# Loading q and k as runs of consecutive tokens over all 128 partitions, nine full transposes each

## The chip, the cores and the metric

One core of one Trainium2 chip runs the whole kernel. The metric is device time in microseconds (us). The kernel before takes 833.95 us, the median of 3 runs (833.22 to 834.21).

## What is computed

Attention over q, k and v of shape (batch 4, heads 8, 576 tokens, head size 64), then a mixture of 8 experts that takes one expert for each token, then a two-layer feed-forward block. Half of the heads look back over 32 tokens (local), the other half at every 32nd token (strided):

```python
scores = scale * np.matmul(q, k.transpose(0, 1, 3, 2))
mask_local = (rel >= 0) & (rel < 32)
mask_strided = (rel >= 0) & (pos[None, :] % 32 == pos[:, None] % 32)
masks = np.stack([mask_local if h < H // 2 else mask_strided for h in range(H)])
attn = softmax(np.where(masks, scores, -1e9))
x = (attn @ v) as rows of tokens               # 2304 x 512
x = _moe_ref(x)                                # top expert of 8, 512 -> 1024 -> 512
out = np.maximum(x @ w_in, 0) ** 2 @ w_out     # 512 -> 2048 -> 512
```

All of it is float32. The change touches the attention alone, which fills the first 165 us of the execution.

## The kernel before

The attention goes batch by batch. `load(b)` issues the transfers of a batch from SyncE's queue (SP): `qs` and `ks` (the four strided heads), `ql` and `kl` with their tails `qlt` and `klt` (the four local heads), `vsp` and `vl` (v for the strided and the local heads). The tiles of q and k have one buffer each, so the next batch's can be loaded only once this batch's have been transposed. `load(1)` is issued ahead of the first batch's scores, and `load(b + 2)` after batch b.

`transposes(b, t)` turns q and k so that the head size lies on the partitions, which the scores need. It yields in 13 groups. A group is a few transposes on TensorE (PE) into one PSUM tile of the pool "tp", which has two buffers, and then one or two copies (`evac`) to `qsT`, `ksT`, `qlT` or `klT`, in turn on ScalarE (ACT) and VectorE (DVE). PSUM tiles are named `ts<b>q`, `ts<b>k` for the strided heads and `tp<b>q`, `tp<b>k`, `tpt<b>` for the local ones. The groups of batch b + 1 are drawn one by one between the units of batch b, by the table `TN`; those of batch 0 at the start.

In `qs` each of 72 partitions holds one head and one run of 32 consecutive tokens (8 KB); in `ql` the tokens lie across the partitions, so that a run in memory is one token's 64 numbers (256 bytes). `piece_s` multiplies, for one residue of the 32, an 18 by 18 block of scores for each head; its PSUM tile is `sc<b>s`. The local units write `sc<b>l`. Behind the scores come the softmax on DVE and ACT (`nm`, `pr`, `sm`, `rc`), another transpose (`pt`), the product with v (`o`) and its copy to `xT`, then the gates (`rw`, `xr`), and stores of x to memory (`x_d`).

The program's order on each engine is set by a scheduler when it is built; each engine then works through its own list in order.

Of the kernel before, what the change touches and what calls it, by code (L numbers as in the profile page):

```python
# [7 lines left out]
F32 = mybir.dt.float32  # L8
# [116 lines left out]
def moe_kernel(ctx, tc, q, k, v, wg, wog, w1, w2, w_in64, w_out64, consts, out, dbg=None):  # L125
# [77 lines left out]
    def turned(pool, i):  # L203
        trs[i] = {}
        for nm in "qk":
            trs[i][nm + "sT"] = pool.tile([P, STRIDE // 2, 4 * SM], F32, name=f"{nm}sT{i}")
            trs[i][nm + "lT"] = pool.tile([P, 2, S], F32, name=f"{nm}lT{i}")

    def padded_v(pool, i):
        vsp[i] = pool.tile([P, 4, 8 * HD], F32, name=f"vsp{i}")  # L210
        nc.gpsimd.memset(vsp[i], 0.0)

    R = 4 * SM
    for nm in "qk":
        qks[nm] = fro.tile([R, STRIDE * HD], F32, name=f"{nm}s")
    turned(fro, B % 2)
    padded_v(big, (B - 1) % 3)
    turned(big, (B - 1) % 2)
# [14 lines left out]
    def load(b):  # L233
        t = {}
        go = nc.sync.dma_start
        if b == 0:
            go = lambda o, i: tc.keep_in_program_order(nc.sync.dma_start(o, i))
        for nm, src in (("q", q), ("k", k)):
            go(qks[nm], src[b, 4:8].rearrange("h (m c) d -> (h m) (c d)", c=STRIDE))
        for nm, src in (("q", q), ("k", k)):  # L240
            x = fro.tile([P, NU, 4, HD], F32, name=f"{nm}l{b}", tag=nm + "l", bufs=1)
            for h in range(4):
                go(x[:, :, h, :], src[b, h, : NU * P].rearrange("(u p) d -> p u d", p=P))
            y = fro.tile([QB, 4, HD], F32, name=f"{nm}lt{b}", tag=nm + "lt", bufs=1)
            go(y, src[b, 0:4, NU * P :].rearrange("h p d -> p h d"))
            t[nm + "l"] = (x, y)
        t["vs"] = x = vsp[b % 3]
        rows = v[b, 4:8].rearrange("h (m i a) d -> i m h (a d)", i=NG, a=8)
        for i in range(NG):
            go(x[32 * i : 32 * i + SM], rows[i])  # L250
        vl = io.tile([KW, 4, NQB, HD], F32, name=f"vl{b}", tag="vl")
        nc.gpsimd.memset(vl[:STRIDE, :, 0, :], 0.0)
        go(vl[STRIDE:, :, 0, :], v[b, 0:4, 0:QB, :].rearrange("h p d -> p h d"))
        for h in range(4):
            base = v[b, h, QB - STRIDE : 2 * QB, :]
            src = bass.AP(base.tensor, base.offset, [[HD, KW], [QB * HD, NQB - 1], [1, HD]])
            last_ld[0] = go(vl[:, h, 1:, :], src)
        t["vl"] = vl
        return t
# [13 lines left out]

    def transposes(b, t):
        t.update(trs[b % 2])
        for c4 in range(STRIDE // 8):
            for nm in ("q", "k"):
                yield
                ps = pss.tile([P, 4, P], F32, name=f"ts{b}{nm}{c4}", tag="tp")
                for i in range(4):  # L280
                    c = (4 * c4 + i) * 2 * HD
                    nc.tensor.transpose(ps[:, i, :R], qks[nm][:, c : c + 2 * HD], ident[:R, :R])
                evac(t[nm + "sT"][:, 4 * c4 : 4 * c4 + 4, :], ps[:, :, :R], 0.125 if nm == "q" else None)
        for hp in range(2):
            for nm in ("q", "k"):
                yield
                ps = pss.tile([P, NU, P], F32, name=f"tp{b}{nm}{hp}", tag="tp")
                for u in range(NU):
                    src = t[nm + "l"][0][:, u, 2 * hp : 2 * hp + 2, :]
                    nc.tensor.transpose(ps[:, u, :], src.rearrange("p h d -> p (h d)"), ident)  # L290
                evac(t[nm + "lT"][:, hp, : NU * P], ps.rearrange("d u p -> d (u p)"), 0.125 if nm == "q" else None)
        yield
        ps = pss.tile([P, 2, 2, QB], F32, name=f"tpt{b}", tag="tp")
        for i, nm in enumerate(("q", "k")):
            for hp in range(2):
                src = t[nm + "l"][1][:, 2 * hp : 2 * hp + 2, :].rearrange("p h d -> p (h d)")
                nc.tensor.transpose(ps[:, i, hp, :], src, ident[:QB, :QB])
        evac(t["qlT"][:, :, NU * P :], ps[:, 0], 0.125)
        evac(t["klT"][:, :, NU * P :], ps[:, 1])

    nun = [0]

# [50 lines left out]
    def piece_s(b, t, u, a):  # L353

        nm = f"{b}s{u}"
        nun[0] += 1
        if a == 0:
            scs[b, u] = pss.tile(G, F32, name=f"sc{nm}", tag="sc")
            nc.tensor.matmul(
                flat(scs[b, u]),  # L360
                identb,
                cstb[:, None, C_MS - C_BF : C_MS - C_BF + SM].to_broadcast([P, n_s, SM]),
                start=True,
                stop=False,
            )
        sc = scs[b, u]
        r = slice(u * HD, (u + 1) * HD)
        for i in range(NG):
            for h in range(4):
                ql, kr = (t[x + "sT"][r, 4 * i + a, SM * h : SM * (h + 1)] for x in "qk")  # L370
                ins = nc.tensor.matmul(sc[32 * h : 32 * h + SM, a, i, :], ql, kr, start=False, stop=(a == i == 3))
        if b == u == 0:
            lead["s0"] = ins
# [369 lines left out]
            scq.append((nun[0] + (SDL if t < GROUPS[1][1] else 0) + i * SCN, lambda i=i, t=t: scatter(i, t)))  # L743

    tg = transposes(0, tiles[0])
    for _ in range(2 * 4 + 1):
        next(tg)
    tiles[1] = load(1)
    nc.gpsimd.memset(zero, 0)
# [3 lines left out]
    for b in range(B):  # L753
        t = tiles[b]
        tn = transposes(b + 1, tiles[b + 1]) if b + 1 < B else iter(())
        for n, ku in enumerate(ORDER[b].split()):
            kind, u = ku[0], int(ku[1:])
            if kind == "l":
                for _ in tg:
                    pass  # L760
                q2.append((b, t, kind, u) + unit(b, t, kind, u))
            else:
                if kind == "b":
                    with tc.issue_after(lead["s0"].ins):
                        next(tg, None)
                piece_s(b, t, "ab".index(kind), u)
                if u == 3:
                    q2.append((b, t, "s", "ab".index(kind)) + unit_s(b, t, "ab".index(kind)))
            drain(D2, D3)
            if b == B - 1 and n >= LN and "do" in lead:  # L770
                lead.pop("do")()
                lead["ok"] = 1
            if b == B - 1 and not early and all(a[0] == b for a in q2 + q3):
                front.close()
                early.append(
                    bulk.enter_context(tc.tile_pool(name="early", bufs=1, side="right", reuse_waits="tile"))
                )
            if scq and nun[0] >= scq[0][0] and (b < B - 1 or "ok" in lead):
                with tc.issue_after(last_ev["p"].ins):
                    scq.pop(0)[1]()  # L780
            for _ in range(TN[b][n]):
                next(tn, None)
        for _ in tn:
            pass
        tg = iter(())
        if b + 2 < B:
            tiles[b + 2] = load(b + 2)
# [649 lines left out]
```

## Time and profile before

| | |
|---|---|
| median of 3 runs | 833.95 us |
| the profiled execution's own time | 826.2 us |
| its span in the profile | 824.4 us |
| PE busy | 772.2 us, 94% |
| DVE busy | 541.8 us, 66% |
| ACT busy | 456.8 us, 55% |
| DMA, mean over the span | 152 GB/s |

The profile is one execution. Busy time of PE is modelled from the pipeline, so a busy PE may still be a waiting one; the clock that TensorE was granted is in the profile as a share of full speed, where 1.00 is 2.4 GHz and 0.50 is 1.2 GHz. A transfer has no row of its own in the timeline: the row on SPq is its issue, and its landing shows as the wait that it ends.

### The profile page before, as it was taken

Reading aid. Unit: us, or ns where it says so; the run is one execution under the profiler, and the core shown is the slowest. Engines: PE = TensorE matmul, PEld = TensorE weight load, DVE = VectorE, ACT = ScalarE, POOL = GpSimd, SP = SyncE. Lnnn points to the kernel's source line nnn. Section 1 sums busy time; section 2 is a strip of 40 time slices with the busy share of each in tenths; the row PEclk is TensorE's granted clock in tenths of the full one; section 3 lists DMA queues with packets and bytes.
Section 4 is the critical chain, followed back from the end, with each engine's and each line's share of the span. In section 5 each row is a group of like instructions: output and inputs, shape, how many; then the busy total and the mean of one; then the engine's idle time right before and its main releaser. Section 6 shows DMA issues by size and latency. Waiting matters only on the chain.

```text
span 824.4 us, 15570 instructions
## 1 busy us (share of the span) xinstructions
PE 772.2 (94%) x5931; PEld 697.3 (85%) x5931; DVE 541.8 (66%) x1025; ACT 456.8 (55%) x928; POOL 198.1 (24%) x186
## 2 busy tenths in 40 slices
PE   4889899859999999999999999999999999999994
PEld 3667677659999999999988889988889988889893
DVE  3445657566545777788899778788565578556542
ACT  1444454324455556566566776686565577456443
POOL 4000312174427665442024212004000003000002
PEclk9797899859999999999999999999999999999998
DMA  8986542074957999887555354335223224312002
GB/s 171 175 178 140 113 99 65 4 233 148 309 181 153 304 254 282 290 279 232 184 190 200 121 203 162 119 119 172 71 90 121 72 89 145 124 71 89 27 1 80
DMA packets 105062, 124.90 MB, mean 152 GB/s; under 512 B 42897, under 2 KB 77233, under 8 KB 104402
## 3 DMA queue, kind: packets, MB, share of 16 engines
q1 hardware_dynamic: 95394, 100.77, 41.8%
q0 software_dynamic: 8096, 22.63, 8.6%
q8 instruction: 48, 0.79, 0.4%
q10 hardware_dynamic: 1488, 0.42, 0.3%
q14 instruction: 36, 0.29, 0.1%
HBM read 101.67 MB, written 22.12 MB: 150 GB/s over the span
## 4 chain that ended last, share of the span: by engine, by line
PE 64%; issue 16%; DMA 8%; DVE 4%; ACT 3%; POOL 3%; SPq 0%; POOLq 0%; ACTq 0%; DVEq 0%
DMA ks<-in_k_dram 5%; PE o L968 5%; PE o L969 5%; PE o L970 5%; PE h L968 4%; PE h L969 4%; PE h L970 4%; PE y L969 4%; PE y L970 4%; PE y L968 4%; PE rw L508 3%; DMA s0wo<-in_moe_w_out_dram 1%; POOL idx_d L860 1%; POOL out_dram L1213 1%; PE wt L1046 1%
## 5 line engine op out<-in xcount | busy, mean ns | idle before, releaser
L968 PE MATMUL o<-hwo,gh 128*128 128x512 f32 x288 | 114.6, 398 | 4.0 <-ACT gh L1096 4.0
L969 PE MATMUL o<-lwo,gh 128*128 128x512 f32 x288 | 113.7, 395 | 0.0
L952 DVE TENSOR_TENSOR lw<-rw,hw 128x1024 fp32r<-128x1024 f32 x62 | 78.4, 1264 | 45.3 <-ACT hw L948 43.5
L948 ACT ACTIVATE hw<-rw 128x1024 fp32r<-128x1024 f32 x62 | 65.9, 1062 | 65.3 <-PE h L969 45.0
L1182 ACT ACTIVATE rl<-rl 128x384 f32<-128x384 f32 x96 | 49.5, 518 | 94.2 <-DVE rl L1180 94.1
L1213 POOL DMA_INDIRECT out_dram<-ob,idx x18 | 20.6, 1147 | 274.1 <-ACT ob L1212 269.4
L970 PE MATMUL o<-hwo,gl 128*128 128x512 f32 x288 | 84.7, 395 | 0.0
L1097 DVE TENSOR_TENSOR gl<-rl,gh 128x384 fp32r<-128x384 f32 x96 | 57.0, 595 | 41.9 <-ACT gh L1096 40.8
L968 PE MATMUL h<-xh,hw 128*128 128x416 f32 (+7 forms) x256 | 80.8, 316 | 1.3 <-DVE hl L1068 0.8
L969 PE MATMUL h<-xl,hw 128*128 128x416 f32 (+7 forms) x256 | 79.4, 310 | 0.2 <-DVE xl L658 0.2
L970 PE MATMUL h<-xh,lw 128*128 128x416 f32 (+7 forms) x256 | 79.5, 310 | 0.0
L969 PE MATMUL y<-hl,hw 128*128 128x416 f32 (+7 forms) x256 | 77.1, 310 | 0.0
L970 PE MATMUL y<-hh,lw 128*128 128x416 f32 (+7 forms) x256 | 76.6, 310 | 0.0
L968 PE MATMUL y<-hh,hw 128*128 128x416 f32 (+7 forms) x256 | 67.9, 310 | 0.0
L968 PEld LDWEIGHTS o<-hwo,gh 128*128 128x128 f32 x288 | 54.3, 189 | 15.8 <-ACT gh L1096 6.6
L970 PEld LDWEIGHTS o<-hwo,gl 128*128 128x128 f32 x288 | 53.7, 188 | 10.3 <-DVE gl L1097 0.4
L969 PEld LDWEIGHTS o<-lwo,gh 128*128 128x128 f32 x288 | 54.3, 189 | 9.0
L1096 ACT ACTIVATE gh<-rl 128x384 fp32r<-128x384 f32 x96 | 49.9, 521 | 1.8
L1183 ACT ACTIVATE rl<-rl 128x384 f32<-128x384 f32 x96 | 49.6, 519 | 1.7
L968 PEld LDWEIGHTS h<-xh,hw 128*128 128x128 f32 x256 | 48.1, 188 | 2.3 <-DVE hl L1068 1.8
L969 PEld LDWEIGHTS h<-xl,hw 128*128 128x128 f32 x256 | 48.2, 188 | 0.5 <-DVE xl L658 0.4
L969 PEld LDWEIGHTS y<-hl,hw 128*128 128x128 f32 x256 | 48.1, 188 | 0.1
(603 smaller groups left out, 1935.5 us busy)
## 6 DMA issues: line engine op xcount, KB each, us to landing
rw<-in_moe_w_dram SPq DMA_DIRECT2D x62, 512.0 KB
rwa<-ws_d SPq DMA_DIRECT2D x24, 512.0 KB
rwb<-ws_d SPq DMA_DIRECT2D x24, 384.0 KB
e6wi<-in_moe_w_in_dram SPq DMA_DIRECT2D x32, 256.0 KB
rwo<-wout_d SPq DMA_DIRECT2D x16, 512.0 KB
x_d<-xr SPq DMA_DIRECT2D x18, 256.0 KB
ws_d<-eo POOLq DMA_DIRECT2D x16, 256.0 KB, 4.8
s0wo<-in_moe_w_out_dram SPq DMA_DIRECT2D x8, 512.0 KB
```

Source lines behind the costliest of these rows:

```text
L508: nc.tensor.matmul(ps[:, kk, :], xT[:, kd, col : col + P], igw[:, kd, :], start=True, stop=True)
L860: ins = nc.gpsimd.indirect_dma_start(out=idx_d[:, :], out_offset=bass.IndirectOffsetOnAxis(ap=cpi[:, t : t + 1], axis=0), in_=toki[:, t, : ...
L948: nc.scalar.activation(hi, raw, AF.Copy)
L952: eng.tensor_tensor(lo, raw, hi.bitcast(F32), op=ALU.subtract)
L968: kept(nc.tensor.matmul(ps, ah, bh, start=first, stop=False))
L969: kept(nc.tensor.matmul(ps, ah, bl_, start=False, stop=False))
L970: kept(nc.tensor.matmul(ps, al, bh, start=False, stop=last))
L1096: nc.scalar.activation(h, x, AF.Copy)
L1097: nc.vector.tensor_tensor(l, x, h.bitcast(F32), op=ALU.subtract)
L1182: nc.scalar.activation(rl[:, :HC], src, AF.Relu)
L1183: nc.scalar.activation(rl[:, :HC], rl[:, :HC], AF.Square)
L1213: ins = nc.gpsimd.indirect_dma_start(out=out[:, :], out_offset=bass.IndirectOffsetOnAxis(ap=idx[:, gt_, 0:1], axis=0), in_=ob, in_offset=None,
```

## The change

The strided q and k of a batch come as one [128, 1152] tile each: a partition holds one head and 18 consecutive tokens (4.5 KB). The local q and k come into one [128, 9, 2, 64] tile each, by four transfers of 64 partitions, with 9 consecutive tokens of one head in a partition (2304 bytes in memory, written as nine pieces of 256 bytes). Both then take nine transposes of 128 by 128, in three groups of three, in place of 16 transposes of 72 rows in four groups for the strided heads and 8 full and 2 short ones in two and a half groups for the local heads. A group's result stands in PSUM in an order that isn't that of the tokens, so the copy writes with a step of nine elements (36 bytes). `qsT` and `ksT` are now in the order of the tokens, and `piece_s` reads both operands with a step of 16 elements (64 bytes). The transfers of v to `vsp` go in the order 0, 2, 1, 3. At the start 7 groups are drawn, where 9 were, and two groups are drawn for each "b" unit of batch 0.

```diff
-            go(qks[nm], src[b, 4:8].rearrange("h (m c) d -> (h m) (c d)", c=STRIDE))
+            t[nm + "s"] = x = fro.tile([P, NS * HD], F32, name=f"{nm}s{b}", tag=nm + "s", bufs=1)
+            go(x, src[b, 4:8].rearrange("h (g n) d -> (h g) (n d)", n=NS))
         for nm, src in (("q", q), ("k", k)):
-            x = fro.tile([P, NU, 4, HD], F32, name=f"{nm}l{b}", tag=nm + "l", bufs=1)
-            for h in range(4):
-                go(x[:, :, h, :], src[b, h, : NU * P].rearrange("(u p) d -> p u d", p=P))
-            y = fro.tile([QB, 4, HD], F32, name=f"{nm}lt{b}", tag=nm + "lt", bufs=1)
-            go(y, src[b, 0:4, NU * P :].rearrange("h p d -> p h d"))
-            t[nm + "l"] = (x, y)
+            t[nm + "l"] = x = fro.tile([P, NL_, 2, HD], F32, name=f"{nm}l{b}", tag=nm + "l", bufs=1)
+            for h in (0, 2, 1, 3):
+                go(x[h // 2 * HD : h // 2 * HD + HD, :, h % 2, :], src[b, h].rearrange("(g n) d -> g n d", n=NL_))
-        for i in range(NG):
+        for i in (0, 2, 1, 3):
             go(x[32 * i : 32 * i + SM], rows[i])
...
-        for c4 in range(STRIDE // 8):
-            for nm in ("q", "k"):
-                yield
-                ps = pss.tile([P, 4, P], F32, name=f"ts{b}{nm}{c4}", tag="tp")
-                for i in range(4):
-                    c = (4 * c4 + i) * 2 * HD
-                    nc.tensor.transpose(ps[:, i, :R], qks[nm][:, c : c + 2 * HD], ident[:R, :R])
-                evac(t[nm + "sT"][:, 4 * c4 : 4 * c4 + 4, :], ps[:, :, :R], 0.125 if nm == "q" else None)
...
+        for kind in "sl":
+            for n0 in range(0, 9, 3):
+                for nm in ("q", "k"):
+                    yield
+                    ps = pss.tile([P, 3, P], F32, name=f"t{kind}{b}{nm}{n0}", tag="tp")
+                    x = t[nm + kind]
+                    for i in range(3):
+                        n = n0 + i
+                        if kind == "s":
+                            src = x[:, 2 * HD * n : 2 * HD * (n + 1)]
+                        else:
+                            src = x[:, n].rearrange("p j d -> p (j d)")
+                        nc.tensor.transpose(ps[:, i, :], src, ident)
+                    y = t[nm + kind + "T"].rearrange("d h (g n) -> d n h g", n=9)[:, n0 : n0 + 3]
+                    heads = 4 if kind == "s" else 2
+                    evac(y, ps.rearrange("d n (h g) -> d n h g", h=heads), 0.125 if nm == "q" else None)
...
-                ql, kr = (t[x + "sT"][r, 4 * i + a, SM * h : SM * (h + 1)] for x in "qk")
+                ql, kr = (t[x + "sT"][r, h].rearrange("d (m c) -> d c m", c=STRIDE // 2)[:, 4 * i + a] for x in "qk")
...
-    for _ in range(2 * 4 + 1):
+    for _ in range(2 * 3 + 1):
         next(tg)
...
                 if kind == "b":
                     with tc.issue_after(lead["s0"].ins):
                         next(tg, None)
+                        next(tg, None)
```

The scheduler puts some instructions at other places as well. On SP, where the transfers of batch 2 are issued, the kernel before has this order (a name is the tile that is written, then its source):

```order
L250 DMA vsp_118<-in_v_dram 18x4x512 x4
L250 DMA vsp_112<-in_v_dram 18x4x512
L239 DMA qs<-in_q_dram 72x2048
L250 DMA vsp_112<-in_v_dram 18x4x512
L239 DMA ks<-in_k_dram 72x2048
L250 DMA vsp_112<-in_v_dram 18x4x512 x2
```

The changed kernel has this order at the same place:

```order
L246 DMA vsp_116<-in_v_dram 18x4x512 x4
L238 DMA qs_664<-in_q_dram 128x1152
L238 DMA ks_666<-in_k_dram 128x1152
L246 DMA vsp_110<-in_v_dram 18x4x512 x4
L249 DMA vl_682<-in_v_dram 64x4x64
```

The second set of four `vsp` transfers, which are batch 3's, stood around `qs` and `ks` of batch 2, two of them ahead of `ks`; now all four stand behind.

On PE, where the first transposes of batch 2 (`ts2q`, `ts2k`) stand between the last units of batch 0, the kernel before has:

```order
L297 MATMUL tpt_701<-cst,klt_221 128x64 x2
L432 MATMUL o0l_886<-pts0l_659,vl_152 64x64
L282 MATMUL ts2q_769<-cst,qs 128x72 x4
L327 MATMUL sc1l_797<-klT_117,qlT_115 64x64 x2
L327 MATMUL sc1l_797<-klT_117,qlT_115 64x96 x4
L432 MATMUL o0l_966<-pts0l_825,vl_152 64x64 x8
L432 MATMUL o0l_1106<-pts0l_884,vl_152 64x64
L282 MATMUL ts2k_791<-cst,ks 128x72 x4
L432 MATMUL o0l_1106<-pts0l_884,vl_152 64x64 x3
L508 MATMUL rw_0_838<-igw,xT 128x144 x2
```

And the changed kernel:

```order
L420 MATMUL o0l_1052<-pts0l_835,vl_148 64x64 x4
L284 MATMUL tl1k_649<-cst,kl_194 128x128 x3
L284 MATMUL tl1q_654<-cst,ql_189 128x128 x3
L284 MATMUL tl1k_659<-cst,kl_194 128x128 x3
L284 MATMUL ts2q_723<-cst,qs_664 128x128 x3
L284 MATMUL ts2k_744<-cst,ks_666 128x128 x3
L315 MATMUL sc1l_749<-klT_115,qlT_113 64x64 x4
L315 MATMUL sc1l_749<-klT_115,qlT_113 64x96 x4
L496 MATMUL rw_0_790<-igw,xT 128x144 x2
```

The eight products of `sc1l` with which the local scores of batch 1 begin stood ahead of `ts2k`, six of them behind `ts2q`; now they stand behind both.

On SP again, where batch 3 begins, the kernel before has:

```order
L528 DMA x_d<-xr_837 512x1x128
L528 DMA x_d<-xr_896 512x1x128
L528 DMA x_d<-xr_976 512x1x128
L239 DMA qs<-in_q_dram 72x2048
L239 DMA ks<-in_k_dram 72x2048
L243 DMA ql_1274<-in_q_dram 128x4x64 x4
```

And the changed kernel:

```order
L516 DMA x_d<-xr_789 512x1x128
L516 DMA x_d<-xr_847 512x1x128
L238 DMA qs_1207<-in_q_dram 128x1152
L516 DMA x_d<-xr_925 512x1x128
L238 DMA ks_1209<-in_k_dram 128x1152
L242 DMA ql_1211<-in_q_dram 64x9x64 x4
```

`qs` of batch 3 has moved ahead of one store of x, and `ks` no longer stands directly behind it.

## Rows read from the trace of the kernel before

**Rows 1.** What PE waited for, 0 to 104 us: total us, times, longest.
```profile
PE ts0q L282 <- DMA cst<-in_consts_dram: 7.0, 1, 7.0
PE ts0k L282 <- DMA ks<-in_k_dram: 2.5, 1, 2.5
PE ts1k L282 <- DMA ks<-in_k_dram: 2.5, 1, 2.5
PE ts3k L282 <- DMA ks<-in_k_dram: 2.5, 1, 2.5
PE ts2k L282 <- DMA ks<-in_k_dram: 2.2, 1, 2.2
PE ts1q L282 <- DMA qs<-in_q_dram: 1.5, 1, 1.5
PE ts2q L282 <- DMA qs<-in_q_dram: 1.3, 1, 1.3
```

**Rows 2.** Chain that ended last: start us, us, what.
```profile
1.23 9.00 DMA ks<-in_k_dram
...
23.56 10.06 DMA ks<-in_k_dram
...
49.49 12.32 DMA ks<-in_k_dram
...
86.80 9.76 DMA ks<-in_k_dram
```

**Rows 3.** Stretches: busy us (instructions) of each engine, granted clock, DMA share, GB/s.
```profile
32.00:43.00 11.00, 9.24 (x87) 7.13 (x88) 3.73 (x9) 3.90 (x13) 1.12 (x2) 0.54 0.85 163
48.00:50.00 2.00, 2.00 (x76) 1.62 (x74) 1.01 (x4) 0.81 (x2) 0.51 (x1) 1.00 0.61 152
59.50:73.00 13.50, 11.31 (x161) 8.94 (x162) 5.14 (x16) 4.96 (x21) 0.97 (x2) 0.51 0.74 157
74.00:88.00 14.00, 13.90 (x219) 11.01 (x220) 12.17 (x45) 9.18 (x37) 2.96 (x3) 1.00 0.31 80
97.00:103.50 6.50, 6.50 (x81) 4.92 (x80) 3.15 (x10) 1.15 (x3) 1.79 (x3) 0.50 0.60 121
```

**Rows 4.** DMA in 13:15 (`ql`, `kl`), 26:31 (`qs`, `ks`) and 166:174 (weights).
```profile
DMA packets 1705, 0.42 MB, mean 212 GB/s; under 512 B 1705, under 2 KB 1705, under 8 KB 1705
...
DMA packets 362, 0.93 MB, mean 187 GB/s; under 512 B 246, under 2 KB 246, under 8 KB 259
...
DMA packets 3227, 2.63 MB, mean 329 GB/s; under 512 B 128, under 2 KB 3063, under 8 KB 3227
```

**Rows 5.** PE's timeline: scores and transposes at full clock.
```profile
58.17 0.66 PE L327 MATMUL sc1l<-klT,qlT 64*64 64x64 f32 x12
...
87.90 0.66 PE L290 MATMUL tp2k<-cst,kl 128*128 128x128 f32 x4
88.48 0.66 PE L371 MATMUL sc2s<-ksT,qsT 64*18 64x18 f32 x58
...
111.56 0.47 PE L282 MATMUL ts3q<-cst,qs 72*128 72x72 f32 x4
```

**Rows 6.** Copies by form, 0 to 190 us: count, busy us and mean ns, idle before.
```profile
L268 DVE COPY klT<-tp3k 128x512 f32<-128x512 f32 x2 | 1.4, 692 | 0.4 <-PE tp3k L290 0.2
L268 DVE COPY xT<-o0s 128x288 f32<-128x288 f32 x2 | 1.3, 664 | 0.3 <-PE o0s L447 0.3
L268 DVE COPY ksT<-ts1k 128x288 f32<-128x288 f32 x2 | 0.9, 458 | 1.8 <-PE ts1k L282 1.8
L272 ACT ACTIVATE xT<-o3s 128x288 f32<-128x288 f32 x2 | 1.4, 679 | 5.4 <-PE sc3l L327 3.6 <-PE o3s L447 1.8
L272 ACT ACTIVATE ksT<-ts2k 128x288 f32<-128x288 f32 x4 | 1.6, 408 | 2.4 <-PE ts2k L282 2.4
L272 ACT ACTIVATE klT<-tp0k 128x512 f32<-128x512 f32 x2 | 1.2, 598 | 4.4 <-PE tp0k L290 4.4
```

More of the change, by code (lines that the diff above doesn't have):

```diff
@@ L205, in turned @@
         for nm in "qk":
-            trs[i][nm + "sT"] = pool.tile([P, STRIDE // 2, 4 * SM], F32, name=f"{nm}sT{i}")
+            trs[i][nm + "sT"] = pool.tile([P, 4, S // 2], F32, name=f"{nm}sT{i}")
             trs[i][nm + "lT"] = pool.tile([P, 2, S], F32, name=f"{nm}lT{i}")
@@ L211, in padded_v @@
         nc.gpsimd.memset(vsp[i], 0.0)
-    R = 4 * SM
-    for nm in "qk":
-        qks[nm] = fro.tile([R, STRIDE * HD], F32, name=f"{nm}s")
+    NS, NL_ = S * 4 // P, S * 2 // P
     turned(fro, B % 2)
@@ L275, in transposes @@
         t.update(trs[b % 2])
-        for c4 in range(STRIDE // 8):
-            for nm in ("q", "k"):
-                yield
-                ps = pss.tile([P, 4, P], F32, name=f"ts{b}{nm}{c4}", tag="tp")
-                for i in range(4):
-                    c = (4 * c4 + i) * 2 * HD
-                    nc.tensor.transpose(ps[:, i, :R], qks[nm][:, c : c + 2 * HD], ident[:R, :R])
-                evac(t[nm + "sT"][:, 4 * c4 : 4 * c4 + 4, :], ps[:, :, :R], 0.125 if nm == "q" else None)
[L284 to L299, printed above, removed]
+        for kind in "sl":
[14 more added lines that the diff above has]
+                    evac(y, ps.rearrange("d n (h g) -> d n h g", h=heads), 0.125 if nm == "q" else None)
     nun = [0]
```

## Prediction

> **What bounds the kernel now.** I read first what TensorE waits for while the attention runs. Its list [rows 1] has one kind of entry that matters: the first transposes of `qs` and `ks` of each batch wait for their transfers. The waits are short, 2.5 + 2.5 + 2.5 + 2.2 + 1.5 + 1.3 us beside the 7.0 us at the very start, so I read the chain next, to see whether they hold up everything. They do: four transfers of `ks` stand on it with 9.0, 10.06, 12.32 and 9.76 us [rows 2], the second and third nearly end to end with other transfers. After 104 us PE no longer waits on q or k.
>
> Then the stretches behind those waits [rows 3]. From 32 to 43, 59.5 to 73 and 97 to 103.5 us the granted clock is 0.54, 0.51 and 0.50, that is 1.2 GHz, each time after PE had stood waiting for `ks`. PE is busy 9.24, 11.31 and 6.50 us there, so a wait costs more than its own length. In 74 to 88 us the clock is 1.00, PE is busy 13.90 of 14 us and DVE 12.17: once the loads are out of the way, PE bounds and DVE is close behind.
>
> Last the transfers themselves [rows 4]. While `ql` and `kl` move, in pieces of 256 bytes, the rate is 212 GB/s; while `qs` and `ks` move, from 72 partitions, it is 187 GB/s, although nearly all the bytes are in large pieces; weights on 128 partitions move at 329 GB/s. The slow transfers are thus the ones that the change spreads over more partitions.
>
> From about 165 us on, the expert and feed-forward phases follow the end of the attention. The change touches nothing there, so I carry what the attention gains to the end of the kernel one to one.
>
> **The loads.** `qs` and `ks` of a batch are 2 x 590 KB = 1.18 MB. At 187 GB/s that is 6.3 us, at the 329 GB/s of a 128-partition transfer 3.6 us [rows 4], so 2.7 us less for each batch. The bounds: no gain at all, if something other than the 72 partitions sets the 187, and 2.7. I take 2.7, since the weights' row has the new shape.
>
> `ql` and `kl` keep their bytes and their pieces of 256 bytes, but a transfer now writes 64 partitions, not 128. Bounds: at 212 GB/s as now, 5.6 us a batch; at the 152 GB/s of the stretch in which `vsp` moves on its few partitions [rows 3], 7.8 us, so up to 2.2 us more. The nearest row is the 187 GB/s of 72 partitions, 6.3 us or +0.7. I take 0, because four transfers that alternate between the halves are in flight one behind the other, and keep +2.2 as the bound.
>
> The Trainium skill speaks against this edit: "SBUF — State Buffer", section "Door 1: The DMA port swizzle", says that a transfer's rate goes by how many of 16 ports its partitions reach, and that 0 to 63 reach only eight, with 196 GB/s measured there for 1 MiB. By that the local loads would take an estimated 6.0 us a batch, 0.4 more than by the row; the rows above agree with it in that 72 partitions move at 187 GB/s.
>
> Until `ks` of batch 2 lands at 61.8 us (49.49 + 12.32, [rows 2]), three batches' `qs` and `ks` pass through the queue: 3 x 2.7 = 8.1 us. Two `vsp` transfers of 144 KB no longer stand ahead of that `ks` on SP; at 152 GB/s [rows 3] each takes 0.97 us, 1.9 in all. So it lands 10.0 us earlier, at about 51.8. Would PE be there by then? It reached `ts2q` at 57.8 − 1.3 = 56.5 us. It now starts earlier by the first of the three 2.7 us, less about 1 because all six groups of `qs` and `ks` must be turned before the first score; it loses the 1.5 + 2.5 us of waits in batch 1; and of the 9.24 busy us at half clock some 4 go. That gives 56.5 − 1.7 − 4 − 4 = 46.8: PE is early, the load still ends last, and a wait with the slow clock behind it stays. I therefore count −10.0 and nothing for 59.5 to 73. The eight products of `sc1l` now stand behind `ts2k`: twelve rows in 0.66 us [rows 5], two rows to a product at this height, so 0.9 us that was done during the wait follows it: +0.9.
>
> For batch 3, `qs` and `ks` were asked for together and `ks` took 9.76 us [rows 2]. Now `qs` goes as soon as the last `ts2q` is done, ahead of a store of x, and `ks` alone remains: 590 KB at 329 GB/s is 1.8 us; doubled for what lies between issue and landing, which is an assumption, it is under 4. PE came to `ts3k` at 96.7 − 2.5 = 94.2 us, 7.4 us after the issue at 86.8. So this wait goes, 2.5 us, and with it the slow clock behind it, half of 6.50 busy us [rows 3], 3.2. Together −5.7. What is late next is DVE and PE themselves.
>
> **The transposes.** Four of 72 rows take 0.47 us, four of 128 by 128 take 0.66 [rows 5]. Before, a batch has 8 groups of the first and 4 of the second and a short one, 8 x 0.47 + 4 x 0.66 + 0.5 = 6.9 us. Now it has 12 groups of three, 12 x 0.50 = 6.0. That is −0.9 a batch; ahead of 52 us the loads cover it, so it counts for two batches: −1.8.
>
> **The copies out with a step.** The trace has one copy that writes with a step, to `xT` (32 elements apart): 288 elements in 664 ns on DVE and 679 on ACT, where 288 without a step take 458 and 408 [rows 6]. That is 0.72 and 0.94 ns more for an element. 384 elements without a step, between the rows for 288 and 512, would be 0.56 and 0.49 us; with it 0.84 and 0.85. Before, a batch has 8 copies of about 0.43, 4 of 0.65 and 2 of 0.28, 6.6 us; now 12 of 0.85, 10.2 us. So +3.6 us a batch over two engines, 1.8 on each. The bounds are 0 (a step of nine costs nothing) and 1.8 a batch. While PE waits for loads it is hidden; behind that, DVE is 87% busy in 74 to 88 [rows 3], and what covers it is thin. I count the whole 1.8 for two batches: +3.6.
>
> The Trainium skill has a higher price. "Vector Engine (DVE) Microarchitecture Reference", section "Measured stream behaviour on trn2", gives 2.50 ns for a column when the output alone steps by 24 words, and 1.05 without. The `xT` row gives about 1.76 instead; by the page's figure a copy would be an estimated 1.1 us and the term about +7, not +3.6. I go by the row.
>
> **The scores with a step.** No row has PE reading an operand with a step. 58 rows of the score products pass in 0.66 us [rows 5], 11 ns each, 22 for a product of 18 columns. A transpose of 128 columns passes in 0.66 / 4 = 165 ns, 1.3 ns a column, so 18 columns would need 23 ns alone, and the products of four heads go to different columns of the array side by side, 6 ns each. The 22 ns are then issue, not reading, and reads could be three times slower before it shows. Bounds: 0, and the 1.67 of the stepped ACT copy [rows 6] on the 1024 rows of the attention, 1024 x 11 ns = 11.3 us, so +7.6. I take 0.
>
> **The sum.** −10.0 + 0.9 − 5.7 − 1.8 + 3.6 = −13.0 us against the profiled execution's 826.2, so 813.2. The median of the runs shown stands 7.75 us above that execution; I carry the same difference: 833.95 − 13.0 = 821.0. A change within 0.2%, about 1.7 us, can't be told from none here.
>
> **The rivals.**
> - *The clock stays up.* If PE no longer waits long for `ks` of batch 2, the 11.31 busy us in 59.5 to 73 shrink by some 5.5. For it: PE waits in several short pieces. Against: by the sum it is 5 us early. 815.
> - *The gain is given back on DVE and in the local loads.* Local loads at 152 GB/s cost 2.2 us for each of two batches ahead of 52 us, +4.4, and copies at twice the added price another 3.6. For it: DVE's 87%. 829.
> - *The loads don't get faster.* If the 187 GB/s come from memory and not from 72 partitions, −8.1 falls away, the third batch's wait shrinks only by the earlier `qs`, and the copies take back the rest: 833 to 834. Against: 329 GB/s on the same queue.
> - *Slower: PE reads with a step at a fraction of its pace.* The place is the 1024 score rows, the price 11.3 us for each whole time by which they get longer. The gain of 13 is gone at 2.15 times, and at three times the kernel takes 833.95 − 13 + 22.6 = 843.5. The page "SBUF — State Buffer" of the Trainium skill says in "Door 1" that each access to a new 16-byte line pays; no row here shows it, and the reckoning of 6 against 22 ns speaks against it.
>
> **How the numbers follow.** The forecast (816 to 827) gets 0.50, the clock that stays up 0.20, the gain given back 0.12, loads no faster 0.08, the slow reads 0.10. Faster takes the first three but a little, 0.82; same the loads' case, 0.07; slower the last and a little, 0.11. The range leaves out the slow reads and the lower end of the second case: 811 to 832.
>
> **What would show it.** Right: the first `ts0k` near 8 us, `ks` of batch 2 landing near 52, no wait at `ts3k` and clock 1.00 behind it, copies to `qsT` near 0.84 us, score rows still 11 ns apart, the attention's end 13 us earlier. Wrong: transfers of `qs` at under 200 GB/s, score rows over 20 ns apart, or DVE so full that waits on copies stand where the waits on loads stood.

## The result, and the profile after

The changed kernel takes 820.15 us (median of 4 runs, 819.81 to 824.56), the kernel before 834.08 us beside it (4 runs, 833.22 to 836.32): ratio 0.9841, 95% interval 0.9803 to 0.988. The forecast was 821.0 us in 811 to 832. The profiled execution of the changed kernel took 819.81 us, with a span of 817.9 us.

What PE waited for from 0 to 104 us (total us, times, longest), to be read against [rows 1]:

```profile
PE ts0q L284 <- DMA cst<-in_consts_dram: 5.8, 1, 5.8
PE sc2s L359 <- issue: 3.4, 6, 1.1
PE ts2k L284 <- DMA ks<-in_k_dram: 2.3, 1, 2.3
PE ts1k L284 <- DMA ks<-in_k_dram: 1.0, 1, 1.0
PE ts0k L284 <- DMA ks<-in_k_dram: 1.0, 1, 1.0
...
PE ts2q L284 <- DMA qs<-in_q_dram: 0.3, 1, 0.3
```

The wait at `ts3k` is gone and those at `ts0k` and `ts1k` fell from 2.5 us to 1.0. The wait at `ts2k` is as long as before. One entry is new: `sc2s` waits 3.4 us for "issue", that is, for nothing that the profile shows.

PE's timeline at the first transposes of `ks` of each batch:

```profile
7.64 0.90 PE L284 MATMUL ts0k<-cst,ks 128*128 128x128 f32 x3 [0.98 <-DMA ks<-in_k_dram]
...
28.86 0.52 PE L284 MATMUL ts1k<-cst,ks 128*128 128x128 f32 x3 [1.04 <-DMA ks<-in_k_dram]
...
51.73 0.87 PE L284 MATMUL ts2k<-cst,ks 128*128 128x128 f32 x3 [2.34 <-DMA ks<-in_k_dram]
...
89.60 0.55 PE L284 MATMUL ts3k<-cst,ks 128*128 128x128 f32 x3
```

The kernel before has at the same places:

```profile
61.95 0.71 PE L282 MATMUL ts2k<-cst,ks 72*128 72x72 f32 x4 [2.19 <-DMA ks<-in_k_dram]
...
96.70 0.68 PE L282 MATMUL ts3k<-cst,ks 72*128 72x72 f32 x4 [2.50 <-DMA ks<-in_k_dram]
```

`ks` of batch 2 lands at 51.73 us, and PE starts on it; before it was 61.95, and the forecast was 51.8. `ts3k` starts at 89.60 us, 96.7 before, with nothing in brackets: it doesn't wait. So a lead of 10 us at `ts2k` is only 7 us at `ts3k`, although a wait has gone between the two. The stretches show where it was lost (columns as in [rows 3]):

```profile
4.00:8.00 4.00, 1.26 (x5) 0.86 (x6) 1.38 (x3) 1.28 (x1) 4.00 (x4) 1.00 1.14 323
...
51.00:58.00 7.00, 6.27 (x92) 5.07 (x93) 2.50 (x7) 3.00 (x11) 0.00 (x0) 0.55 0.75 170
59.50:73.00 13.50, 13.50 (x228) 10.50 (x227) 10.44 (x39) 9.89 (x40) 1.53 (x2) 1.00 0.75 178
74.00:88.00 14.00, 10.48 (x184) 7.70 (x181) 5.03 (x12) 4.13 (x8) 3.97 (x4) 0.76 0.20 55
...
97.00:103.50 6.50, 6.50 (x100) 5.14 (x98) 4.90 (x15) 4.18 (x16) 0.90 (x2) 1.00 0.45 121
```

In 4 to 8 us, where the first loads of q and k stand, all transfers together move at 323 GB/s (226 before). The clock is at its lower level, 1.2 GHz, from 51 to 58 us, half as long as the stretch of 59.5 to 73 us that stood there before, and at 1.00 from 97 to 103.5 us, where it was 0.50. In 74 to 88 us, where PE had been busy 13.90 of 14 us [rows 3], it is busy 10.48 us at a granted clock of 0.76. PE's timeline inside that stretch:

```profile
75.55 0.62 PE L359 MATMUL sc2s<-ksT,qsT 64*18 64x18 f32 x35
76.63 0.27 PE L359 MATMUL sc2s<-ksT,qsT 64*18 64x18 f32 x4 [0.46 <-issue]
77.38 0.27 PE L359 MATMUL sc2s<-ksT,qsT 64*18 64x18 f32 x5 [0.48 <-issue]
78.10 0.26 PE L359 MATMUL sc2s<-ksT,qsT 64*18 64x18 f32 x5 [0.46 <-issue]
78.82 0.28 PE L359 MATMUL sc2s<-ksT,qsT 64*18 64x18 f32 x5 [0.46 <-issue]
79.55 0.47 PE L359 MATMUL sc2s<-ksT,qsT 64*18 64x18 f32 x24 [0.45 <-issue]
```

Here PE starves: four or five score rows, then half a microsecond of nothing, again and again. What POOL does meanwhile, from its own timeline:

```profile
73.89 1.16 POOL L717 DMA_INDIRECT tab_d<-tok,posi  x1 [0.83 <-DVE posi L684]
75.35 0.98 POOL L717 DMA_INDIRECT tab_d<-tok,posi  x1 [0.30 <-issue]
76.63 0.97 POOL L717 DMA_INDIRECT tab_d<-tok,posi  x1 [0.30 <-issue]
77.91 0.97 POOL L717 DMA_INDIRECT tab_d<-tok,posi  x1 [0.30 <-issue]
```

These are the scatters of token numbers into the experts' table, one for each 128 tokens. PE starves until 0.7 us after the last of them has ended, and waits once more, 1.1 us, up to 83.5 us. The next group, five scatters from 128.52 us on, has the same beside it, in `sc3s` and `rw`. In the profile of the kernel before, the scatters start at 85.5 and 135.56 us, and PE doesn't starve there.

The copies by form (count, busy us and mean ns):

```profile
L266 DVE TENSOR_SCALAR qsT<-ts0q 128x384 f32<-128x384 f32 x3 | 2.6, 852 | 2.4 <-PE ts0q L284 2.4
...
L268 ACT ACTIVATE ksT<-ts2k 128x384 f32<-128x384 f32 x3 | 2.6, 867 | 3.9 <-PE ts2k L284 3.9
```

Over all groups the mean lies between 844 and 897 ns on DVE and between 854 and 927 on ACT; 0.84 and 0.85 us were forecast. The score rows of `sc2s`, from PE's timeline where nothing interrupts them:

```profile
92.71 1.08 PE L359 MATMUL sc2s<-ksT,qsT 64*18 64x18 f32 x82
```

That is 13.2 ns a row, where it was 11.4 ([rows 5], 58 rows in 0.66 us).

### The profile page after: what moved, and what is told of

Same layout as the page of the kernel before. It is cut to its first block, busy times and chain, and to the rows that moved or that the text cites. A ratio compares the mean times of both kernels' runs of the same rounds, so it can differ in the third digit from the quotient of the medians.

```text
span 817.9 us, 15418 instructions
## 1 busy us (share of the span) xinstructions
PE 771.9 (94%) x5867; PEld 693.2 (85%) x5867; DVE 541.6 (66%) x1021; ACT 463.7 (57%) x924; POOL 199.0 (24%) x186
## 4 chain that ended last, share of the span: by engine, by line
PE 52%; issue 17%; ACT 3%; DMA 3%; POOL 3%; DVE 3%; POOLq 0%; SPq 0%; DVEq 0%; ACTq 0%
PE o L957 5%; PE o L959 5%; PE o L958 5%; PE h L957 4%; PE y L957 4%; PE y L958 4%; PE y L959 4%; PE h L958 4%; PE h L959 4%; DMA s0wo<-in_moe_w_out_dram 2%; DMA win<-x_d,ix 1%; PE lr L636 1%; POOL out_dram L1202 1%; PE wt L1035 1%; POOL idx_d L849 1%
## 5 line engine op out<-in xcount | busy, mean ns | idle before, releaser
L959 PEld LDWEIGHTS h<-xh,lw 128*128 128x128 f32 x256 | 48.1, 188 | 0.1
```

Source lines behind the costliest of these rows:

```text
L959: kept(nc.tensor.matmul(ps, al, bh, start=False, stop=last))
```

## The experiments

The theory was the prediction's: the strided loads come faster from 128 partitions, that and the wait at `ts3k` make the gain, the stepped copies give some of it back, and the local part costs nothing. Kernels that are told together ran on one chip and share the runs of the kernel before.

**The two halves of the change, the order of the copies, and the kernel before again.** One kernel is the kernel before, with no edit. One has the strided part alone, of which these are the lines:

```diff
-            go(qks[nm], src[b, 4:8].rearrange("h (m c) d -> (h m) (c d)", c=STRIDE))
+            t[nm + "s"] = x = fro.tile([P, NS * HD], F32, name=f"{nm}s{b}", tag=nm + "s", bufs=1)
+            go(x, src[b, 4:8].rearrange("h (g n) d -> (h g) (n d)", n=NS))
...
+                y = t[nm + "sT"].rearrange("d h (g n) -> d n h g", n=9)[:, n0 : n0 + 3]
+                evac(y, ps.rearrange("d n (h g) -> d n h g", h=4), 0.125 if nm == "q" else None)
```

One has the local part alone:

```diff
-            for h in range(4):
-                go(x[:, :, h, :], src[b, h, : NU * P].rearrange("(u p) d -> p u d", p=P))
+            for h in (0, 2, 1, 3):
+                go(x[h // 2 * HD : h // 2 * HD + HD, :, h % 2, :], src[b, h].rearrange("(g n) d -> g n d", n=9))
```

And one has the whole change, but each copy writes three neighbouring elements before it steps; the step of 128 elements is then in what it reads from PSUM:

```diff
-                    y = t[nm + kind + "T"].rearrange("d h (g n) -> d n h g", n=9)[:, n0 : n0 + 3]
+                    y = t[nm + kind + "T"].rearrange("d h (g n) -> d h g n", n=9)[:, :, :, n0 : n0 + 3]
...
-                    evac(y, ps.rearrange("d n (h g) -> d n h g", h=heads), 0.125 if nm == "q" else None)
+                    evac(y, ps.rearrange("d n (h g) -> d h g n", h=heads), 0.125 if nm == "q" else None)
```

> The kernel before, unchanged, for a second profile. The two profiles that are there differ by 6.5 us of span (824.4 and 817.9), the timed runs by 13.9 us. If the first profile caught an unusually short execution, this one has a span near 832 us, and its waits on ks and the slow clock behind them are longer than in the first. If a profiled execution is always shorter than a timed one, the span is 824 to 826 again.

> The kernel before with the new form for the strided q and k alone (one transfer over 128 partitions, nine transposes, copies and score operands with a step); the local ones and the order of v as before. If the loads of qs and ks over 128 partitions carry the gain, this has 9 to 13 of the 13.9 us: 821 to 825 us, and ks of batch 2 lands near 52 us. If the fewer and larger transposes or the local loads carry it, it has half or less: 827 us or more.

> The kernel before with the new form for the local q and k alone (four transfers of 64 partitions each, nine transposes, copies with a step); the strided ones as before. If the strided loads carry the gain, this is within 3 us of the kernel before, 831 to 837 us, and PE still waits some 2 us for ks in batches 1 to 3. If the local part carries it, 827 us or less; if 64 partitions slow the loads, 837 us or more.

> The changed kernel with the copies walking the same elements in another order: three adjacent elements are written in a row, and the step lies in what is read from PSUM. If it is the written step that makes a copy of 384 elements take 0.85 us, the copies fall towards 0.56 us on DVE and 0.49 us on ACT, and of the 3.6 us counted for them some come back: 816 to 819 us. If a step costs the same on the reading side, nothing changes: 819 to 821 us, copies still near 0.85 us.

Measured, beside a kernel before of 830.91 us (23 runs): the kernel before again 828.07 us, ratio 0.9978 (0.9952 to 1.0004); the strided part alone 819.19 us, 0.9856 (0.9814 to 0.9898); the local part alone 831.36 us, 1.0016 (0.9988 to 1.0044); runs of three 812.76 us, 0.9771 (0.9737 to 0.9805). So the strided part carries the gain and the local part is worth nothing that can be measured. In the strided part alone `ks` of batch 2 lands at 54.90 us, not near 52, and the time is still below the 821 to 825 us that I expected.

The second profile of the kernel before has a span of 827.6 us, between the two values that I had set against each other. Its waits on `ks` are not longer than in the first (2.4, 1.5, 1.1 and 1.6 us); that on `qs` of batch 2 is (3.7 us).

What the local part leaves in place is seen in its waits from 0 to 104 us:

```profile
PE ts0k L279 <- DMA ks<-in_k_dram: 2.9, 1, 2.9
PE ts1q L279 <- DMA qs<-in_q_dram: 2.8, 1, 2.8
```

I had expected that it also waits some 2 us for `ks` in batches 1 to 3. It waits 0.3 us in batch 1 and not at all in the other two, because PE comes there later; its row at `ts2k`, and the stretch of 43 to 51 us, where the kernel before has the clock at 1.00:

```profile
66.14 0.74 PE L279 MATMUL ts2k<-cst,ks 72*128 72x72 f32 x4
...
43.00:51.00 8.00, 8.00 (x85) 6.40 (x83) 3.35 (x10) 3.11 (x14) 0.83 (x1) 0.57 1.07 166
```

So a wait that has gone isn't a gain by itself.

Runs of three looked like 7 us gained over the changed kernel, and the copies were indeed shorter (554 to 594 ns on DVE). But that compares two chips, and in this kernel's profile PE doesn't starve at the scatters of `sc2s` and `sc3s`. Nor does it in the other three, but for one wait of 0.4 us in `sc2s` of the strided part and one of 2.1 us on "issue" in the local kernel, which ends at 92.96 us, 1.9 us after the last scatter of its first group. Whether the copies or the starving made the 7 us was open.

**Each strided load as two halves; the changed kernel again; the strided part with runs of three.** The first is the changed kernel with this edit:

```diff
-            go(x, src[b, 4:8].rearrange("h (g n) d -> (h g) (n d)", n=NS))
+            for h in (0, 2):
+                go(x[32 * h : 32 * h + 64], src[b, 4 + h : 6 + h].rearrange("h (g n) d -> (h g) (n d)", n=NS))
```

The second has no edit. The third is the strided part alone with the copies' edit from above.

> The changed kernel with each of its strided transfers (128 partitions, 590 KB) cut into two of 64 partitions, asked for one behind the other; nothing else differs. Theory of the prediction (the number of partitions of one transfer sets its rate): 64 partitions move no faster than the 72 of before, so qs and ks of a batch take about 6 us again, ks of batch 2 lands some 8 us later than in the changed kernel (near 59 us, with a wait of several us at ts2k), and the time is 826 to 830. Rival (two transfers on different partitions that stand one behind the other share the queue's engines, so the rate is set by what is in flight together): the rate of the stretch stays near that of the changed kernel, ks of batch 2 lands within 2 us of it, and the time is 818 to 823. This would also be why the local loads, which are in halves already, cost nothing.

> The changed kernel, unchanged, for a second profile. If the stall at 76 to 84 us (PE between score rows, waiting for nothing that the profile shows, next to POOL's scatter) comes from this program's order, it is there again, with DVE's instructions there released late too; if it comes from where an instruction fetch happened to meet the scatter, it lies elsewhere or is gone. The time should be 820 within 4.

> The strided part alone (local loads and their transposes as in the kernel before), with the copies out going through three neighbouring elements before they step. If the gain of the strided part (0.986) and of the runs of three (0.9771 against 0.9841) lie in different terms and add, the ratio is 0.980 to 0.983, about 817; only the strided copies profit here, half of those that step in the whole change. If the local part with runs of three gains something of its own (fewer transposes and fewer copies), this comes out slower than the 812.8 of the whole change with runs of three; if the local part costs, it comes out at or below it.

Measured, beside a kernel before of 836.47 us: halves 828.62 us, 0.9902 (0.9871 to 0.9934); the changed kernel again 823.69 us, 0.9854 (0.9824 to 0.9885); the strided part with runs of three 829.92 us, 0.9912 (0.9882 to 0.9943).

The time of the halves is what the prediction's theory expected, its place only in part. PE's timeline of the halves:

```profile
10.29 0.87 PE L285 MATMUL ts0k<-cst,ks 128*128 128x128 f32 x3 [1.74 <-DMA ks<-in_k_dram]
...
53.90 0.70 PE L285 MATMUL ts2k<-cst,ks 128*128 128x128 f32 x3 [2.02 <-DMA ks<-in_k_dram]
```

At the first load, which stands first in SP's queue, the rate of all transfers from 4 to 8 us is 235 GB/s, where the changed kernel has 323 (320 when it ran again), and `ts0k` starts 2.65 us later: the 2.7 us of the forecast. But `ks` of batch 2 lands 2.2 us later than in the changed kernel's first profile, 4.1 later than in its second, not 8.

The traces keep a record of every DMA packet, and those of `qs` and `ks` are known by their size. From the first to the last of them these microseconds pass:

| | batch 0 | batch 1 | batch 2 |
|---|---|---|---|
| kernel before, its two profiles | 7.7, 7.6 | 8.2, 7.4 | 10.6, 12.8 |
| halves | 7.2 | 6.6 | 7.7 |
| changed kernel, its two profiles | 5.2, 4.6 | 6.1, 4.2 | 7.7, 5.9 |

So one transfer over all partitions beats two halves by 2 us at the first load; at the later ones the two profiles of the changed kernel lie some 2 us apart themselves, and the halves take 0.5 us more than the first of them or as long. And the halves keep 836.47 − 828.62 = 7.9 of the 12.8 us that the changed kernel gains beside them. Not all of the 4.9 us between the two is the loads': PE starves beside the scatters here too, and waits 3.8 us more on "issue" up to 89.75 us.

The Trainium skill, page "SBUF — State Buffer", section "Door 1: The DMA port swizzle", says that partitions 0 to 63 reach half of the ports that all 128 reach, so that a transfer to them alone goes at about half the rate. The trace agrees in direction: 235 against 323 GB/s, with two halves on different ports one behind the other.

The starving came again in all three kernels, always beside the scatters of `sc2s` and `sc3s`. The strided part with runs of three, which should have been faster than the strided part alone, was slower by the ratio (0.9912 against 0.9856). Its PE at the scatters that start at 82.9 us:

```profile
85.67 0.29 PE L372 MATMUL sc2s<-ksT,qsT 64*18 64x18 f32 x5 [0.48 <-issue]
86.44 0.26 PE L372 MATMUL sc2s<-ksT,qsT 64*18 64x18 f32 x5 [0.47 <-issue]
87.19 0.29 PE L372 MATMUL sc2s<-ksT,qsT 64*18 64x18 f32 x5 [0.48 <-issue]
```

That pointed away from the copies, to the starving. The new theory: the scatters starve PE, in some programs or on some chips, and the 7 us were that.

**The scatters left out.** Nine of the 18 scatters are left out, in the changed kernel, in the one with runs of three and in the strided part with runs of three; runs of three ran again unchanged. The experts then gather row 0 in place of the rows that these scatters would have named:

```diff
-            scq.append((nun[0] + (SDL if t < GROUPS[1][1] else 0) + i * SCN, lambda i=i, t=t: scatter(i, t)))
+            scq.append((nun[0] + (SDL if t < GROUPS[1][1] else 0) + i * SCN, lambda i=i, t=t: scatter(i, t) if t >= GROUPS[1][1] else None))
```

> The changed kernel without the scatters of the first nine 128-token tiles (nine of POOL's 18, in two groups, during sc2s and sc3s); the table keeps its zeros there, so the experts gather row 0 in their place and the output is not the reference's. PE's order is the same. In the profiles of the changed kernel PE starves between score rows from some 2.5 us after the first scatter of either group until 0.7 us after the last. Theory: that stall, not the copies, is what separates it from the kernel with runs of three. Then the stalls at 76 and 132 us are gone, sc2s and sc3s last some 24 and 22 us (27 and 28 before), and the ratio is 0.975 to 0.980 (0.985 with them). Rival: the copies' step itself holds up PE, the starving only shows where: sc2s and sc3s stay at 27 and 28 us, and the ratio stays at 0.983 to 0.987.

> The same nine scatters left out of the kernel with runs of three, which shows no such stall. Theory of the stall: nothing is gained but POOL's time, ratio 0.975 to 0.979 as with all scatters, and within 2 us of the changed kernel without these scatters plus what the copies are worth (at 0.29 us a copy, 3.5 us a batch over two engines, 0 to 3.6 us in all). Rival: if the scatters cost every kernel alike, it gains as much as the changed kernel does, 5 us or more.

> The kernel with runs of three, unchanged, a second time and beside the others. If the absence of the stall belongs to the program, it is absent again and the ratio is 0.974 to 0.980; if it was chance of that execution, the stall at the scatters appears and the ratio comes near the changed kernel's 0.985.

> The strided part alone with runs of three, which showed the stall (sc2s 33 us, sc3s 28 us) and 0.9912, without the same nine scatters; the output is changed in the same way. Theory of the stall: the stalls go, sc2s takes some 24 us and sc3s some 22, and the ratio falls to 0.978 to 0.984, at or below the strided part alone with stepped copies (0.9856, no stall). Rival: something else made it slower than the strided part alone, and it stays over 0.988.

Measured, beside a kernel before of 836.38 us: the changed kernel with few scatters 808.50 us, 0.9669 (0.9623 to 0.9715); runs of three with few scatters 808.12 us, 0.9654 (0.9613 to 0.9694); runs of three again, with all of them, 824.80 us, 0.9852 (0.9815 to 0.9889); the strided part with runs of three and few scatters 817.32 us, 0.978 (0.9729 to 0.9831).

Runs of three again is the telling one. The kernel that took 812.76 us takes 824.80 here, and its PE now does this at its scatters (from 72.64 us on):

```profile
76.14 0.28 PE L359 MATMUL sc2s<-ksT,qsT 64*18 64x18 f32 x5 [0.49 <-issue]
76.87 0.28 PE L359 MATMUL sc2s<-ksT,qsT 64*18 64x18 f32 x6 [0.45 <-issue]
77.61 0.28 PE L359 MATMUL sc2s<-ksT,qsT 64*18 64x18 f32 x6 [0.46 <-issue]
```

So the starving doesn't belong to the program: the same kernel shows it in one profile and not in the other, which were taken on two chips. I had expected that its absence would repeat, and that the runs of three gain nothing from fewer scatters; both were wrong. They gain 16.7 us, about as much as the changed kernel, as the rival had it. Without the nine scatters no kernel's PE starves in `sc2s`. From the first expert product `h` to the end of the span, the changed kernel and runs of three again take 636.7 and 636.9 us, and 637.8 and 638.2 with few scatters: the gain stands ahead of the experts and doesn't come from what they gather. The copies' step is then worth 808.50 − 808.12 = 0.4 us, and the intervals of the two ratios, some 4 us to either side, overlap nearly whole.

The 16.7 us are not all starving. On the chip where runs of three showed none, it took 812.76 us with all scatters, 4.6 us more than with few; the rest, some 12 us, is an estimate for the starving, from runs on two chips. In its profile there the clock is low from 88 to 97 us, where both kernels with few scatters have it at 1.00; nine busy microseconds at 0.50 are 4.5 us, about the 4.6. Why it fell there is not shown.

```profile
88.00:97.00 9.00, 9.00 (x93) 7.25 (x93) 4.04 (x13) 3.00 (x12) 2.05 (x3) 0.50 1.08 198
```

**The kernel before without the same nine scatters.** The same edit; it tells what the starving takes from the kernel before, whose two profiles don't show it.

> The kernel before without the same nine scatters of POOL; the output is changed in the same way. In the two profiles of the kernel before PE doesn't starve at the scatters of sc2s and sc3s, but in both they were taken where its time was 826 to 828 us, and its median on the other chips is 834 to 836. Without these scatters the changed kernel takes 808.5 us (0.9669 of the kernel before with them). Theory A (the starving takes from the changed kernel alone): the kernel before gains nothing here, ratio 0.996 to 1.002, and the change is worth some 3% where the scatters don't disturb it. Theory B (it takes from both, most where PE is fuller): ratio 0.985 to 0.995, and the change is worth some 2.2 to 2.7% without it. Theory C (it takes as much from the kernel before): ratio 0.979 to 0.985, and the change is worth the 1.6% that was measured, with or without the scatters.

Measured: 823.64 us (6 runs), beside a kernel before of 835.99 us; ratio 0.9844 (0.9817 to 0.9871). That is theory C, at its edge to B: the kernel before gains 12.4 us, the changed kernel gained 15.2 (823.69 to 808.50, on two chips). Without the nine scatters the change is worth 823.64 − 808.50 = 15.1 us, or 0.9669 / 0.9844 = 0.982, as with them (0.9841 and 0.9854).

The two kernels with few scatters, each on its own chip, are the pair in which the change can be read undisturbed. PE's timeline, the kernel before with few scatters:

```profile
10.49 0.74 PE L282 MATMUL ts0k<-cst,ks 72*128 72x72 f32 x4 [2.50 <-DMA ks<-in_k_dram]
...
63.74 0.71 PE L282 MATMUL ts2k<-cst,ks 72*128 72x72 f32 x4 [1.18 <-DMA ks<-in_k_dram]
...
94.80 0.44 PE L282 MATMUL ts3k<-cst,ks 72*128 72x72 f32 x4 [1.44 <-DMA ks<-in_k_dram]
...
141.34 0.38 PE L371 MATMUL sc3s<-ksT,qsT 64*18 64x18 f32 x30
...
186.37 0.46 PE L968 MATMUL h<-xh,hw 128*128 128x416 f32 x1 [0.27 <-ACT xh L657]
```

The changed kernel with few scatters:

```profile
7.25 0.90 PE L284 MATMUL ts0k<-cst,ks 128*128 128x128 f32 x3 [0.92 <-DMA ks<-in_k_dram]
...
51.00 0.55 PE L284 MATMUL ts2k<-cst,ks 128*128 128x128 f32 x3 [0.61 <-ACT klT L268]
...
79.60 0.55 PE L284 MATMUL ts3k<-cst,ks 128*128 128x128 f32 x3
...
124.58 0.43 PE L359 MATMUL sc3s<-ksT,qsT 64*18 64x18 f32 x22
...
168.93 0.36 PE L957 MATMUL h<-xh,hw 128*128 128x416 f32 x1
```

The lead grows from 3.2 us at `ts0k` to 12.7 at `ts2k`, 15.2 at `ts3k` and 16.8 at the last scores; the first expert product `h` starts 17.4 us earlier. The profiled execution of this kernel before took 827.5 us, the slowest of its six and 3.9 above its median, so these leads are rather too long. The pair also tells why the copies cost so little. The changed kernel with few scatters in 74 to 88 us:

```profile
74.00:88.00 14.00, 14.00 (x305) 11.01 (x305) 9.12 (x22) 7.58 (x25) 2.27 (x4) 1.00 0.78 130
```

PE is busy all 14 us, DVE 9.12 and ACT 7.58. PE alone bounds this stretch. Behind the loads, from 52 us on, PE waits for one copy of q or k, `klT` of batch 3, for 0.3 us, and for the same 0.3 us with runs of three (the 0.6 us for `klT` ahead of `ts2k` stand where runs of three waits 0.9 us for the load):

```profile
PE tl3k L284 <- DVE klT L264: 0.3, 1, 0.3
```

## Why the prediction was right, step by step

**The loads, −10.0: right in size.** PE starts on `ks` of batch 2 10.2 us earlier in the changed kernel's profile, 12.7 in the undisturbed pair. The three batches' `qs` and `ks` were on the way for 26.6 us before and 19.0 in the profile after, 7.6 less where 8.1 was forecast (27.8 and 14.6 in the second profiles). The working was off in one place: 187, 329 and 323 GB/s are rates of all transfers in a stretch, on more than one queue. By their own packets the first `qs` and `ks` move at 152 GB/s before (1.18 MB in 7.7 us) and 228 after. That the number of partitions of one transfer does all this is not shown: in the halves the three loads still take 21.4 us in sum. What else makes them faster, the order of the transfers among other things, is open.

**The slow clock behind that wait: half right.** I said that it stays. It does, but for 7 us and not 13.5 (0.55 from 51 to 58 us). PE busy 6.27 us at 0.55 loses 2.8 us there, where 11.31 busy us at 0.51 lost some 5.5 [rows 3], so 2.7 us came on top. When the changed kernel ran again, the clock stayed at 1.00 there behind a wait of 1.4 us. So the first rival holds in part, and was rightly priced as one that ends lower. With few scatters PE doesn't wait for that load at all and the clock stays at 1.00, but there the clock had been low ahead of it, from 20 to 32 us:

```profile
20.00:32.00 12.00, 11.04 (x88) 8.31 (x86) 7.05 (x17) 6.31 (x23) 0.82 (x1) 0.53 1.00 232
```

**The wait at `ts3k`, −5.7: right.** No wait, and clock 1.00 behind it in 97 to 103.5 us.

**The transposes, −1.8: too large.** A group of three takes 0.55 us at full clock, forecast 0.50. By the forecast's own sum that is 12 x 0.55 = 6.6 us a batch against 6.9, so −0.6 for two batches. The +0.9 us for `sc1l` was not measured by itself.

**The copies, +3.6: the term that was mis-sized.** Their duration was right to 0.1 us, their cost on the path was not. PE's waits show none of it behind the loads beyond what the short copies cost too, and the times show 0.4 us (with intervals too wide to exclude 3.6 by themselves). I counted them because DVE was 87% busy in 74 to 88 us, but a copy costs only if PE comes to wait for it, and where PE bounds a stretch it does not. In the Trainium skill, "Vector Engine (DVE) Microarchitecture Reference", "Measured stream behaviour on trn2", has two rules for this. Its price for one stepped output, an estimated 1.1 us a copy, was too high by the rows (0.85). Its rule that runs of two or more adjacent words go at the full rate holds for runs that start on an 8-byte boundary; of the runs of three every second one doesn't, and yet they take 0.55 to 0.59 us for 384 elements, what was forecast without a step.

**The stepped score reads, 0: a little low.** 13.2 ns a row against 11.4, over the 1024 rows 1.8 us. The reckoning that reads could be three times slower before it shows was too kind; the rival of slow reads, which needs more than twice the time, fell.

**The local loads, 0: right.** 1.0016 by themselves. The rival that they give the gain back fell with this, and so did the one that the loads don't get faster, by the first load's 5.2 us in place of 7.7.

With these sizes, and the copies at 0, the sum is −10.2 − 2.7 + 0.9 − 5.7 − 0.6 + 1.8 = −16.5 us; the undisturbed pair ends its scores 16.8 us apart and has medians 15.1 us apart. So the forecast of −13.0 was 2 to 4 us short: the copies and half of the slow clock, less the transposes and the score reads.

**The step that was right by luck** is the base. I carried the 7.75 us between the profiled execution of the kernel before and its median over to the changed kernel as something that neither kernel changes. The sum gave 813.2 us for the profiled execution, and it took 819.8. The changed kernel's profile and its median agree within 0.4 us, and the two profiled executions lie only 6.4 us apart. The likeliest reading is that the starving at the scatters is in the median of the kernel before, and not in its profile, but in both of the changed kernel's. That the scatters cost the kernel before 12.4 us is shown; that they starve PE there was never seen in a profile of it. Since they take about as much from either kernel, the carried difference came out right.

No kernel here is shown to be faster than the changed kernel with all the work done: where PE starves, runs of three (0.9852) and the changed kernel (0.9854) are the same.

## What to carry to other kernels

A load that a stretch waits for is worth spreading over all partitions, and its gain is best read from where PE starts on it, since a shorter wait also shortens the slow clock behind it. A copy that gets longer costs next to nothing as long as PE alone bounds the stretch, however busy its engine looks. And a gain of one per cent between two kernels that ran on different chips is not yet a gain: run both again side by side, above all when one profile has a stall that the other lacks.

## What was not expected of the hardware

PE starved beside GpSimd's indirect scatters: 4 to 6 score rows each 0.72 to 0.77 us, where a row otherwise takes 13 ns, from about 2 to 3 us after a group's first scatter to 0.7 to 1.2 us after its last, with a granted clock of 0.50 behind it from 80 to 85 us when the changed kernel ran again. It came in the profile after and in all profiles of the second and third group of runs that had all scatters; in the four of the first group the pattern is absent. With nine scatters left out, 12.4 to 16.7 us went. By what way a scatter holds up PE, and why one profile shows it and another of the same kernel doesn't, stays open; that it is the chip is one reading, and each chip had one profile of a kernel. Single waits on "issue" also stand far from any scatter: 2.67 us at 63.16 us in the local kernel, 1.90 us at 17.57 us in the strided part with few scatters. The order of PE's instructions was the same in the changed kernel and in the one with runs of three. That the scatters be put elsewhere, with all the work done, wasn't tried.

PE's instructions are a candidate, since nothing that the profile shows holds it. The Trainium skill, "Runtime: NRT & Kernel Launch", section "Instruction fetch mechanics", says that each engine's instructions are streamed in blocks of 16 KiB, mostly hidden; the profile after has 48 such transfers with 0.79 MB in one queue, which agrees with the size of a block. From 76 to 78 us one of them passes in the profile after, where PE starves, and one in the first profile of runs of three, where it doesn't; no run here shows whether they come late.
